# Windowed attention in block-diagonal 64-key tiles, rows divided and then transposed, in front of a squared-ReLU feed-forward layer

## The chip, the cores and the metric

The kernel runs on one core of one Trainium2 chip. The metric is device time in microseconds (us), the median of several executions.

A core has five engines that each work off their own list of instructions: TensorE (PE in the profile; its weight loads are PEld), VectorE (DVE), ScalarE (ACT), GpSimd (POOL) and SyncE (SP; here it only issues transfers). Transfers run on 16 DMA engines. The "granted clock" is the TensorE clock in parts of full speed, as the profile records it.

## The reference

There are 8 batches of 8 heads, 576 positions each, head size 64. A position attends to positions at most 32 away. The result, as 4608 tokens of 512, goes through a feed-forward layer with a squared ReLU.

```python
scores = q @ k.T / sqrt(64)
mask   = abs(pos[:, None] - pos[None, :]) <= 32
attn   = softmax(where(mask, scores, -1e9))
x      = (attn @ v)            # then (batch, position, head*64): 4608 x 512
h      = x @ w_in              # 512 -> 2048
g      = s * maximum(h, 0)**2 + b
out    = g @ w_out             # 2048 -> 512, float32
```

The kernels compute `b` apart: `g @ w_out = s*(r*r @ w_out) + b*colsum(w_out)`. The column sum is a vector that is needed before the first output row.

## The kernel before

Everything is bf16 on TensorE. The work comes as tasks, each with a stream (its engine), a guessed cost, the tiles that it reads and writes, and a priority `key`. A small planner in the kernel's own program goes through the tasks as a simulated machine would and so fixes, when the kernel is built, one order of instructions for each engine. Nothing in the program changes these orders later: each engine is given its list as it stands, with waits at semaphores in it. The costs in the planner therefore cost no time themselves; they only decide orders.

```python
# the planner: take the task that can start first; ties go by key
for s in self.STREAMS:
    for t in open_[s]:
        c = (max(free[s], t.ready), t.key, t.n)
        if best is None or c < best[0]:
            best = (c, t)
...
if t.dma is not None:                       # one queue for all transfers
    dma_free = max(dma_free, st + 1300.0) + t.dma[1]
    t.fin = dma_free + 700.0
```

Attention goes in units of 192 queries and two pairs of heads, six units a batch. Per unit: scores (keys stationary), exp, a mask multiply, then two groups of matmuls with the probabilities moving: one with a matrix of ones (the row sums) and one with V. The sums come out in the layout of the result, so log, exp(-x) and a multiply give x already transposed for the feed-forward layer.

```python
add("act", exp(SC) -> EX)                       # 128 x 1024
add("dve", EX *= MASK)
for (dst, res) in ((SS, "SS"), (AV, "AV")):     # ones, then V, stationary; EX moving
    add("pe", 8 matmuls: dst[64*hh:..., ...] <- lhsT = ONES or VB, rhs = EX)
add("act", LNS = ln(SS));  add("act", REC = exp(-LNS))
add("dve", XT = AV * REC)
# ... a unit of batch b > 0 may not be planned before a chosen feed-forward step:
r = 32 + 6 * (i - 3) - 7 + 3 * g2               # cut: i counts 192-row blocks
after = [("s1", r // 16, r % 16)]
```

q, k and v are loaded as float32, cast on VectorE, and q and k are transposed by DMA (by TensorE for batch 0). The feed-forward layer goes in blocks of tokens, 384, 128 and then 512 each: `s1` is x times `w_in`, ScalarE does the ReLU, VectorE the square, `s2` is the second matrix, VectorE scales and adds, SyncE stores.

The softmax here doesn't subtract the row's maximum and nothing guards it: scores larger than these inputs give would overflow.

## Time and profile before

| | before |
|---|---|
| time, median of 3 runs | 371.59 us (369.63 to 373.37) |
| span of the profiled execution | 373.8 us |
| TensorE busy | 319.2 us |
| ScalarE / VectorE / GpSimd busy | 206.4 / 193.2 / 44.7 us |

First the page of the kernel before: the busy line, and the span in 40 slices (each digit is a busy share in tenths; PEclk is the granted clock).

```profile
PE 319.2 (85%) x2385; PEld 155.5 (42%) x2424; DVE 193.2 (52%) x439; ACT 206.4 (55%) x310; POOL 44.7 (12%) x62
PE   1277985935499999988898899989999999999996
PEclk9999998975599999999999999999999999999999
DMA  8979999999999999999899798863000001001012
```

TensorE is idle at the start and in a hole at slices 9 to 11, where its clock falls too; DMA is nearly full until slice 27 (about 250 us) and then idle. The same by stretches of time: for each stretch its length, then the busy time of each engine with its count of instructions, the granted clock, the DMA share and GB/s.

```profile
0.00:34.00 34.00, 14.42 (x151) 9.33 (x152) 15.55 (x44) 14.08 (x20) 6.75 (x17) 1.00 1.01 164
80.00:106.00 26.00, 14.36 (x135) 8.09 (x137) 15.21 (x34) 13.51 (x20) 5.99 (x7) 0.56 1.20 222
140.00:240.00 100.00, 92.34 (x786) 43.89 (x797) 63.42 (x145) 70.84 (x105) 10.18 (x12) 1.00 1.06 186
```

And the hole, in TensorE's timeline (start, duration, what, and the idle time before it with what ended it):

```profile
84.11 0.64 PE L458 MATMUL ss<-ex,ones 128*64 128x128 bf16 x8 [2.03 <-DVE ex L445]
84.54 0.63 PE L458 MATMUL av<-ex,vb 128*64 128x128 bf16 x8
85.11 0.61 PE L435 MATMUL sc<-qt,kt 64*128 64x128 bf16 x8
87.65 0.64 PE L458 MATMUL ss<-ex,ones 128*64 128x128 bf16 x8 [1.93 <-DVE ex L445]
```

One unit every 3.6 us, nothing else to run: TensorE waits for the exp and mask of each unit, and there is no feed-forward work because block 2 needs batch 1. The Trainium skill ("TensorE: Matmul & The Clock Gate", section "HAM oscillation — how this bites in real kernels") says that idle gaps of TensorE of more than some 3.4 us bring its clock down; here pauses of 2 us between bursts of some 1.6 us already go with a granted clock of 0.56.

### The profile page before, as it was taken

To read this page: it belongs to the slowest core of one execution; us is meant where nothing else is said; L and a number is where in the kernel's file an instruction comes from. 1 tells how busy PE (TensorE), PEld (TensorE's weight loads), DVE (VectorE), ACT (ScalarE), POOL (GpSimd) and SP (SyncE) were. 2 spreads that over 40 slices of the span, in tenths; PEclk is the share of its full clock that TensorE was granted. 3 is DMA by queue.
4 is the path that set the end of the run, shared out by engine and by line. 5 is a ranking of instruction groups with operands and counts; after the bars stand their busy time and mean duration, and the time that the engine had idled before them with its cause. 6 is when DMAs were issued, how large, how long until landed. Compare 5 with 4: busy or idle time off the path is not lost.

```text
span 373.8 us, 6108 instructions
## 1 busy us (share of the span) xinstructions
PE 319.2 (85%) x2385; PEld 155.5 (42%) x2424; DVE 193.2 (52%) x439; ACT 206.4 (55%) x310; POOL 44.7 (12%) x62
## 2 busy tenths in 40 slices
PE   1277985935499999988898899989999999999996
PEld 0144543523244444443444344434444444444442
DVE  4363525745556775676585586454444453333321
ACT  1266732255368678767677576657676764434300
POOL 3012241342221210121111000000000000000000
PEclk9999998975599999999999999999999999999999
DMA  8979999999999999999899798863000001001012
GB/s 164 208 110 187 190 225 206 202 190 213 230 221 147 180 200 231 186 198 193 188 172 213 132 174 174 189 141 89 28 31 31 28 30 56 28 30 56 28 58 84
DMA packets 127869, 52.71 MB, mean 141 GB/s; under 512 B 116672, under 2 KB 120768, under 8 KB 127840
## 3 DMA queue, kind: packets, MB, share of 16 engines
q1 hardware_dynamic: 113648, 36.32, 54.2%
q0 software_dynamic: 7424, 14.29, 19.8%
q10 hardware_dynamic: 6768, 1.70, 2.7%
q8 instruction: 19, 0.31, 0.4%
q14 instruction: 10, 0.08, 0.1%
HBM read 38.80 MB, written 9.44 MB: 129 GB/s over the span
## 4 chain that ended last, share of the span: by engine, by line
PE 54%; DMA 19%; SPq 9%; DVE 7%; ACTq 3%; ACT 3%; issue 2%; DVEq 0%
PE o L543 25%; PE w L525 22%; DMA stgq<-in_q_dram 12%; DMA stgk<-in_k_dram 7%; SPq L300 6%; ACTq L300 3%; SPq L387 3%; PE ss L458 3%; PE sc L435 2%; DVE ex L445 2%; PE av L458 2%; ACT ex L442 1%; DVE xt L472 1%; DVE vb L379 1%; DVE gt L534 1%
## 5 line engine op out<-in xcount | busy, mean ns | idle before, releaser
L525 PE MATMUL w<-xt,win 128*128 128x512 bf16 (+2 forms) x624 | 146.4, 367 | 5.5 <-DVE xt L472 4.2
L543 PE MATMUL o<-wout,gt 128*128 128x512 bf16 x554 | 141.5, 382 | 6.0 <-DVE cvec L567 4.0
L525 PEld LDWEIGHTS w<-xt,win 128*128 128x128 bf16 x640 | 59.4, 100 | 71.8 <-issue 5.1
L543 PEld LDWEIGHTS o<-wout,gt 128*128 128x128 bf16 x576 | 53.2, 98 | 65.5 <-DVE cvec L567 4.2
L442 ACT ACTIVATE ex<-sc,zero 128x1024 bf16<-128x1024 f32 x48 | 53.2, 1109 | 12.1 <-PE sc L435 12.1
L445 DVE TENSOR_TENSOR ex<-ex,mask 128x1024 bf16<-128x1024 bf16 x48 | 33.0, 688 | 33.2 <-ACT ex L442 32.7
L300 POOL DMA_DIRECT2D stgv<-in_v_dram x42 | 35.7, 853 | 120.5 <-DVE vb L379 111.5
L465 ACT ACTIVATE lns<-ss,zero 128x384 f32<-128x384 f32 x48 | 27.7, 578 | 27.6 <-PE ss L458 27.5
L531 ACT ACTIVATE r_29<-w,zero 128x512 bf16<-128x512 f32 (+2 forms) x40 | 25.7, 643 | 30.7 <-PE w L525 30.6
L458 PE MATMUL ss<-ex,ones 128*64 128x128 bf16 x384 | 22.1, 244 | 20.5 <-DVE ex L445 20.1
L531 ACT ACTIVATE r_28<-w,zero 128x512 bf16<-128x512 f32 (+2 forms) x40 | 25.7, 642 | 23.1 <-PE w L525 22.6
L531 ACT ACTIVATE r_31<-w,zero 128x512 bf16<-128x512 f32 (+2 forms) x40 | 25.7, 644 | 23.0 <-PE w L525 22.0
L531 ACT ACTIVATE r_30<-w,zero 128x512 bf16<-128x512 f32 (+2 forms) x40 | 25.7, 643 | 19.2 <-PE w L525 18.8
L555 DVE SCALAR_TENSOR_TENSOR outs<-o,sb_36,cvec 128x512 f32<-128x512 f32 x36 | 26.8, 746 | 13.2 <-PE o L543 12.8
L472 DVE TENSOR_TENSOR xt<-av,rec 128x384 bf16<-128x384 f32 x48 | 26.5, 552 | 11.5 <-ACT rec L468 11.2
L379 DVE CAST natq<-stgq 128x512 bf16<-128x512 f32 (+1 forms) x40 | 17.2, 432 | 25.3 <-DMA stgq<-in_q_dram 25.0
L458 PEld LDWEIGHTS ss<-ex,ones 128*64 128x64 bf16 x384 | 13.6, 119 | 39.6 <-DVE ex L445 26.7
L468 ACT ACTIVATE rec<-lns,zero 128x384 f32<-128x384 f32 x48 | 29.3, 610 | 0.8
L435 PE MATMUL sc<-qt,kt 64*128 64x128 bf16 x384 | 21.2, 237 | 9.0 <-ACT qt L407 5.3
L534 DVE TENSOR_TENSOR gt<-r_29 128x512 bf16<-128x512 bf16 (+2 forms) x40 | 15.8, 396 | 22.7 <-ACT r_29 L531 22.7
L534 DVE TENSOR_TENSOR gt<-r_31 128x512 bf16<-128x512 bf16 (+2 forms) x40 | 15.8, 396 | 22.3 <-ACT r_31 L531 22.0
L534 DVE TENSOR_TENSOR gt<-r_30 128x512 bf16<-128x512 bf16 (+2 forms) x40 | 15.8, 394 | 18.6 <-ACT r_30 L531 18.6
(43 smaller groups left out, 134.4 us busy)
## 6 DMA issues: line engine op xcount, KB each, us to landing
out_dram<-outs SPq DMA_DIRECT2D x36, 256.0 KB, 2.3
stgq<-in_q_dram SPq DMA_DIRECT2D x31, 256.0 KB, 5.8
stgk<-in_k_dram SPq DMA_DIRECT2D x29, 256.0 KB, 6.0
stgv<-in_v_dram POOLq DMA_DIRECT2D x28, 256.0 KB, 5.7
stgv<-in_v_dram POOLq DMA_DIRECT2D x14, 192.0 KB, 5.9
win<-in_moe_w_in_dram POOLq DMA_DIRECT2D x4, 512.0 KB, 6.4
wout<-in_moe_w_out_dram POOLq DMA_DIRECT2D x4, 512.0 KB, 5.8
stgq<-in_q_dram SPq DMA_DIRECT2D x8, 128.0 KB, 5.9
```

The costliest lines, as they stand in the source:

```text
L300: lambda e: e.dma_start(STG[n][p0:p1, blk, :].rearrange("p (h d) -> p h d", h=H), src_of[n][b, :, s0:s0 + ns, :].rearrange("h s d -> s h d ...
L435: fns.append(lambda e, u=u, pr=pr, a=a, hh=hh: e.matmul(SC[:, hh, 256 * u + 128 * a:256 * u + 128 * a + 128], lhsT=KT[slot][64 * hh:64 * h ...
L442: add("act", lambda e: e.activation(EX[e_][:, :, :], SC[:, :, :], AF.Exp, bias=ZERO_F[:, :], scale=0.125), 1130.0, reads=["SC", "ZERO"], w ...
L445: add("dve", lambda e: e.tensor_tensor(EX[e_][:, :, :], EX[e_][:, :, :], MASK[:, :, :], ALU.mult), 700.0, reads=[("E", e_), "MASK"], write ...
L458: fns.append(lambda e, u=u, a=a, hh=hh, dst=dst, lhs=lhs: e.matmul(dst[64 * hh:64 * hh + 64, 192 * u + 64 * a:192 * u + 64 * a + 128], lhs ...
L465: add("act", lambda e: e.activation(LNS[e_][:, :], SS[:, 0:384], AF.Ln, bias=ZERO_F[:, :], scale=1.0), 600.0, reads=["SS", "ZERO"], writes ...
L468: add("act", lambda e: e.activation(REC[e_][:, :], LNS[e_][:, :], AF.Exp, bias=ZERO_F[:, :], scale=-1.0), 600.0, reads=[("LNS", e_), "ZERO ...
L472: add("dve", lambda e: e.tensor_tensor(XT[:, prs[0]:prs[1] + 1, x0:x0 + 192], AV[:, 0:384].rearrange("p (u c) -> p u c", u=2), REC[e_][:, ...
L525: add("pe", [lambda e, kc=kc: e.matmul(W[wb][:, 0:nt], lhsT=WIN_BF[:, kc, ft * 128:(ft + 1) * 128], rhs=XT[:, kc, t0:t0 + nt], start=(kc = ...
L531: add("act", lambda e: e.activation(R1[rb][:, 0:nt], W[wb][:, 0:nt], AF.Relu, bias=ZERO_F[:, :], scale=1.0), 280 + 0.82 * nt, reads=[("W", ...
L534: add("dve", lambda e: e.tensor_tensor(GT[gs][:, ft, 0:nt], R1[rb][:, 0:nt], R1[rb][:, 0:nt], ALU.mult), 160 + 0.53 * nt, reads=[("R1", rb ...
L543: add("pe", [lambda e, fc=fc: e.matmul(O[ob][:, :], lhsT=GT[gs][:, fc, sub * 128:sub * 128 + 128], rhs=WOUT_BF[:, fc, :], start=(fc == 0), ...
```

## The change

The intent is fewer and fuller instructions for attention. Keys and V of two heads are put into block-diagonal 128 x 128 tiles of 64 keys (`KBD`, `VBD`), zero elsewhere. In the second product the probabilities are now the stationary operand and V moves, with a column of ones beside it for each head; so sums and results arrive together, with queries on partitions. A reciprocal of 8 columns and one multiply divide the rows; the result `XN` is then transposed, by TensorE for batch 0, by DMA for the others. V is loaded straight into `VBD` with a cast in the transfer. A batch has five units (128 keys, all heads) in place of six. The column sum moves from TensorE to GpSimd. The first token block has 128 tokens. The pins that tie attention to a feed-forward step are gone; every task has a due time instead, and the planner's model of the DMA gets two queues and new constants.

```diff
-    sizes = [384, 128]
+    sizes = [128, 384]
...
-                dma_free = max(dma_free, st + 1300.0) + t.dma[1]
-                t.fin = dma_free + 700.0
+                me = "sw" if t.stream == "pool" else "hw"
+                other = ring["hw" if me == "sw" else "sw"]
+                at = max(ring[me], st + t.cost + 500.0)
+                ring[me] = at + t.dma[1] + min(t.dma[1], max(0.0, other - at) / 2)
+                t.fin = ring[me] + 1100.0
...
+        def due(b, m):                      # cut: when block of unit m should start
+            return PH[blk] - 14.0 - (1.0 - f) * before
...
+                # q, k of a 128-row chunk, batches 1 to 7
+                add("sp", load STG,  600.0, key=key - 20 + 0.1 * i, ...)
+                add("dve", NAT = cast(STG), 620.0, key=key)
+                add("sp", QT, KT = transpose(NAT), 1250.0, dma=("t", ns * 6.5), key=key)
+                add("dve", KBD = KT in blocks, 260, key=key)
...
-                for (dst, res) in ((SS, "SS"), (AV, "AV")): ...   # ones and V stationary
-            add("act", ... AF.Ln ...);  add("act", ... AF.Exp, scale=-1.0)
-            add("dve", XT = AV * REC)
+                    fns.append(matmul(AVN[0:nr, pr, 0:130], lhsT=EX[...], rhs=VBD[slot][:, j, pr, 0:130]))
+            add("dve", REC = reciprocal(AVN[:, :, 128:130]), 220)
+            add("dve", XN = AVN * REC, 680)
+                add("sp", lambda e: e.dma_start(XT[:, :, x0:x0 + nr], XN[xi][0:nr, :], transpose=True),
+                    1250.0, reads=[("XN", xi)], writes=[("XT", b, m)], key=key, dma=("t", nr * 6.5))
...
-                        r = 32 + 6 * (i - 3) - 7 + 3 * g2
-                        after = [("s1", r // 16, r % 16)]
```

## The prediction

> **What bounds the kernel now.** By time, three different things. The chain of waits and the windows give: 0 to 32 us, no feed-forward matmul runs (loads and the first attention units); 32 to 60 us, TensorE is busy 23 of 28 us and waits for the column-sum vector, whose weights land late because weight loads queue behind batch 0; 75 to 99 us, TensorE is busy 9 of 24 us at a granted clock of 0.58: six attention units of batch 1 run one after the other, about 3.5 us each (exp 1.11, mask 0.69, sums, log 0.58, exp 0.61, multiply 0.55), with no feed-forward work left to fill in. From 99 to 240 us TensorE is busy 94% beside DMA engines that are nearly full; after 240 us it is the only limit. Necessary TensorE work, from start-to-start times in the timeline: 1152 feed-forward matmuls, four in 0.86 us, = 249 us; 48 attention units at about 0.75 us = 36 us; column sum 3.4; transposes about 2: near 291 us of a 374 us span. So about 80 us is loss, two thirds of it before 100 us.
>
> **What the change does to each engine.** TensorE: attention becomes 36 + 52 matmuls of about 128 columns a batch. The trace issues 128-column matmuls, each with new weights, every 55 ns, so 4.9 us a batch, 39 us in all: no gain over 36. The output transposes of batch 0 add 1 to 2 us, the column sum saves 2.5. Total stays near 294 us. ScalarE: log and reciprocal-exp (28 + 29 us) go, exp falls from 53 to some 37 us; it was not the limit except in the serial units. VectorE: V casts (20 us) go, key-block copies and reciprocals come: about equal. GpSimd: 15 adds; the Trainium skill ("GPSIMD Engine Reference", Elementwise) gives 2.6 cycles an element, an estimate of 1.1 us each against the 0.7 that the schedule assumes; no trace here shows it yet. DMA: V is read once, not 1.22 times, already cast; but 35 more DMA transposes come, an estimate of 0.8 to 0.9 us of DMA time each. Per batch some 30 us of DMA against some 36 us of TensorE: nearly full, still hidden.
>
> **The gain is the order, not the arithmetic.** The first block has 128 tokens, weights start at once, attention is placed by due times a block ahead, and 5 units a batch replace 6. I expect the first feed-forward matmul near 20 us (was 31.9), no wait like that of 75 to 99 us (about 20 us back), a shorter wait for the column sum (about 5), some waits left near 45 to 60 us while batch 1 loads beside the weights. Then TensorE runs nearly solid: 20 + 285 + 18 of waits + 5 of drain = 328 us.
>
> **Prediction:** 328 us, 8 in 10 between 312 and 349. Faster by over 2%: 0.95; within 2%: 0.03; slower: 0.02.
>
> **What would show it.** Right: first feed-forward matmul before 24 us; TensorE busy about 90% from 60 us on with the clock at full; ScalarE busy down by about 65 us; VectorE within 10%; attention matmuls about 55 ns apart; GpSimd adds over 1 us. Wrong, if TensorE has a wait of over 10 us after 60 us.
>
> **What would make it wrong.** V's cast load writes 128-byte pieces; if it takes twice the estimated DMA time, DMA binds to the end (345 us or more). The SyncE queue now issues 105 transposes at 1.2 us each, the outputs and all q and k loads in one fixed order, and an output transpose waiting at its head blocks the rest. Slow weight loads for 96-row tiles would add a few us. If all this stays hidden, 312 us.

## The result and the profile after

| | before | after |
|---|---|---|
| time, median (4 runs each) | 372.48 us (369.63 to 377.95) | 386.25 us (385.54 to 386.79) |
| ratio | | 1.039, 95% interval 1.033 to 1.046 |
| span of the profiled execution | 373.8 us | 385.0 us |
| first feed-forward matmul | 31.9 us | 33.8 us |
| start of block 2 (needs batch 1) | 98.8 us | 106.3 us |
| start of block 6 | 229.8 us | 246.4 us |

A ratio is the mean time of one kernel's runs over that of the other's of the same rounds, so not quite the ratio of the medians. Executions over 1.5% slower than the fastest of the same kernel are left out of the means. The kernel became 3.9% slower where 12% less was predicted. The same views as before:

```profile
PE 312.3 (81%) x1948; PEld 167.6 (44%) x1982; DVE 200.5 (52%) x463; ACT 130.1 (34%) x220; POOL 86.4 (22%) x108
PE   3137396971298779887999599999999999999996
PEclk9999699996579989999899799999999999999999
DMA  9999999859968996999889987592121111101012
```

```profile
0.00:34.00 34.00, 11.96 (x98) 9.52 (x99) 15.77 (x39) 9.84 (x12) 32.55 (x46) 1.00 1.31 189
80.00:106.00 26.00, 7.59 (x66) 4.85 (x65) 11.25 (x26) 3.37 (x5) 6.25 (x8) 0.69 1.18 153
140.00:240.00 100.00, 89.41 (x532) 45.82 (x542) 59.43 (x143) 35.29 (x57) 12.45 (x16) 0.94 1.03 172
```

The work did shrink: ScalarE's busy time fell by 76 us, TensorE's by 7. But the hole at 80 to 106 us got deeper (7.6 us of TensorE work in place of 14.4), and the pauses between 140 and 240 us did not close: 10.6 us of pauses where the kernel before had 7.7, now with a clock of 0.94. The loss can be put in three parts: the time before 34 us, TensorE's busy time after it (the sum over the stretches less the first), and the rest.

| us | before | after |
|---|---|---|
| until 34 us | 34 | 34 |
| TensorE busy after 34 us | 304.7 | 300.3 |
| TensorE idle after 34 us | 35.1 | 50.7 |

So the 11.2 us that the span grew by are 15.6 us more idle time, less 4.4 us of work. (In both traces 1 to 2% of the matmul records are missing, 2385 matmuls beside 2424 weight loads before and 1948 beside 1982 after, so the split is good to some microseconds only.)

Where does the idle time come from? What VectorE waited for between 60 and 300 us (total, times, longest, in us). First the kernel before, then after; only the waits for transfers are shown.

```profile
DVE natq L379 <- DMA stgq<-in_q_dram: 13.9, 14, 2.2
DVE natk L379 <- DMA stgk<-in_k_dram: 8.8, 10, 2.0
```

```profile
DVE kbd L429 <- DMA kt<-nat: 22.1, 16, 3.6
DVE nat L420 <- DMA stg<-in_k_dram: 20.5, 14, 2.4
DVE xn L496 <- DMA xt<-xn: 7.1, 7, 2.1
```

What do these waits hold up? Block 2 of the feed-forward layer needs the transposed results of units 0 to 3 of batch 1. Unit 3's rows (`xn`) were ready at 88.66 us. This is what SyncE issues then (start, duration, what):

```profile
88.62 0.57 SPq L393 DMA_DIRECT2D stg<-in_k_dram  x1
...
90.61 1.81 SPq L424 DMA_TRANSPOSE qt<-nat  x1
92.47 1.39 SPq L424 DMA_TRANSPOSE kt<-nat  x1
93.90 1.27 SPq L512 DMA_TRANSPOSE xt<-xn  x1
...
97.53 2.86 SPq L576 DMA_DIRECT2D out_dram<-outs  x1
100.43 1.23 SPq L512 DMA_TRANSPOSE xt<-xn  x1
```

The transpose of unit 2 goes out at 93.90 (its rows were ready 10.7 us before), that of unit 3 at 100.43, 11.8 us late: in SyncE's list, five loads, a pair of transposes for batch 2, unit 2's late transpose and a store stand in front of it. It lands at 106.2 us, and only then block 2 can start. VectorE's list, too, has prefetch in front of due work. VectorE is only 52% busy, so a wait there looks harmless; what stands behind it decides:

```profile
90.46 0.20 DVE L493 RECIPROCAL rec<-avn 96x8 f32<-96x8 f32 x1
91.97 0.75 DVE L420 CAST nat<-stg 128x1024 bf16<-128x1024 f32 x1 [1.30 <-DMA stg<-in_k_dram]
92.64 0.67 DVE L470 TENSOR_TENSOR ex<-ex,mask 128x1024 bf16<-128x1024 bf16 x1
95.22 0.69 DVE L420 CAST nat<-stg 128x1024 bf16<-128x1024 f32 x1 [1.91 <-DMA stg<-in_k_dram]
99.56 0.59 DVE L429 COPY kbd<-kt 64x512 bf16<-64x512 bf16 x2 [3.65 <-DMA kt<-nat]
100.95 0.69 DVE L496 TENSOR_TENSOR xn<-avn,rec 96x512 bf16<-96x512 f32 x1 [0.80 <-DMA xt<-xn]
```

The reciprocal of unit 4, the last of batch 1, is done at 90.66 us. The multiply that makes `xn` from it comes ten microseconds later. Two casts and a pair of copies for batch 2, each waiting for a transfer, stand before it in the list. But they alone do not set this time: at the end the multiply waits 0.80 us more for its buffer. There are two `XN` buffers, and unit 2's transpose, issued late at 93.90, holds this one until it lands; without the casts and copies the multiply would have stood as long. Here it is SyncE's list that binds (such waits are the 7.1 us of `xn L496` above). Whether VectorE's list would hold the multiply by itself can be seen only beside another list on SyncE (section 5 of the experiments). The Trainium skill ("PSUM — Partial Sum Buffer", section "Engine vs sequencer instructions") says that the queues of ScalarE, VectorE and GpSimd are strictly first in, first out; no trace here shows an exception. TensorE in the same stretch:

```profile
89.05 0.62 PE L485 MATMUL avn<-vbd,ex 128*96 128x130 bf16 x8
97.76 1.03 PE L451 MATMUL sc<-qt,kbd 128*128 128x128 bf16 x8 [8.09 <-DMA qt<-nat]
101.69 1.10 PE L485 MATMUL avn<-vbd,ex 128*96 128x130 bf16 x8 [2.90 <-DVE xn L496]
106.26 3.59 PE L544 MATMUL w<-xt,win 128*128 128x512 bf16 x8 [3.47 <-DMA xt<-xn]
```

It waits for a transpose of batch 2 that its own list has next, then for VectorE's late `xn` (which still holds the PSUM tile), then for SyncE's late `xt`: 14.5 us in three pieces.

From 40 to 240 us SyncE is busy issuing for some 19 of every 20 us (18.8 to 19.6): a transpose keeps it 1.26 us in the median (1.40 in the mean, 105 of them), a load 0.59. The outcome is that the plan and the chip drift apart. The kernel's own planner, with the constants that it has, ends at 338 us, with the transpose of unit 3 of batch 1 issued at 74.1 us; on the chip it is issued at 100.4.

Two theories:

- **Orders.** The change's instructions are good, but the orders were planned with transfers that land too early. On the chip the lists of VectorE, SyncE and TensorE then put prefetching, and work that waits for it, in front of work that is due.
- **Amounts (the rivals).** The change simply added too much of something: 35 more DMA transposes on SyncE, V in 128-byte pieces (packets of the software queue rose from 7,424 to 42,112, and the time that they took from 19.8% to 29.0% of the 16 engines' span), weights that block batch 1's loads.

### The profile page after: what moved, and what is told of

The parts are those of the page before. It is cut to its first block, busy times and chain, and to the rows that moved or that the text cites. A ratio compares the mean times of both kernels' runs of the same rounds, so it can differ in the third digit from the quotient of the medians.

```text
span 385.0 us, 5293 instructions
## 1 busy us (share of the span) xinstructions
PE 312.3 (81%) x1948; PEld 167.6 (44%) x1982; DVE 200.5 (52%) x463; ACT 130.1 (34%) x220; POOL 86.4 (22%) x108
## 3 DMA queue, kind: packets, MB, share of 16 engines
q0 software_dynamic: 42112, 8.92, 29.0%
## 4 chain that ended last, share of the span: by engine, by line
PE 51%; DMA 21%; SPq 13%; POOL 7%; DVE 5%; issue 2%; ACT 1%; POOLq 0%; DVEq 0%; ACTq 0%
PE o L561 23%; PE w L544 22%; DMA xt<-xn 7%; SPq L424 7%; DMA stg<-in_k_dram 7%; PE avn L485 4%; DMA kt<-nat 4%; POOL vbd L380 3%; SPq L393 3%; DMA win<-in_moe_w_in_dram 3%; SPq L512 2%; POOL csum L582 2%; PE sc L451 2%; DVE gt L552 1%; DVE nat L420 1%
## 5 line engine op out<-in xcount | busy, mean ns | idle before, releaser
L550 ACT ACTIVATE r<-w 128x512 bf16<-128x512 f32 (+2 forms) x160 | 88.4, 554 | 173.2 <-PE w L544 143.5
L552 DVE TENSOR_TENSOR gt<-r 128x512 bf16<-128x512 bf16 (+2 forms) x160 | 66.5, 424 | 64.9 <-ACT r L550 64.3
L380 POOL DMA_DIRECT2D vbd<-in_v_dram x64 | 49.4, 800 | 168.0 <-PE avn L485 132.6
L485 PE MATMUL avn<-vbd,ex 128*128 128x130 bf16 (+1 forms) x416 | 35.2, 241 | 19.8 <-DVE ex L470 10.4
L468 ACT ACTIVATE ex<-sc 128x1024 bf16<-128x1024 f32 (+2 forms) x48 | 36.4, 773 | 42.8 <-PE sc L451 38.8
L485 PEld LDWEIGHTS avn<-vbd,ex 128*128 128x128 bf16 (+1 forms) x416 | 30.6, 117 | 30.4 <-DVE ex L470 14.4
L420 DVE CAST nat<-stg 128x1024 bf16<-128x1024 f32 (+1 forms) x35 | 25.3, 722 | 26.6 <-DMA stg<-in_k_dram 26.5
L451 PE MATMUL sc<-qt,kbd 128*128 128x128 bf16 (+1 forms) x288 | 23.5, 226 | 14.0 <-DMA qt<-nat 12.3
L470 DVE TENSOR_TENSOR ex<-ex,mask 128x1024 bf16<-128x1024 bf16 (+2 forms) x48 | 25.1, 529 | 17.7 <-ACT ex L468 17.2
L429 DVE COPY kbd<-kt 64x512 bf16<-64x512 bf16 (+1 forms) x70 | 21.0, 300 | 22.6 <-DMA kt<-nat 22.1
L573 DVE SCALAR_TENSOR_TENSOR outs<-o,sb,cvec 128x512 f32<-128x512 f32 x36 | 26.8, 745 | 11.2 <-PE o L561 11.2
L496 DVE TENSOR_TENSOR xn<-avn,rec 128x512 bf16<-128x512 f32 (+1 forms) x40 | 27.4, 686 | 7.6 <-DMA xt<-xn 7.1
L451 PEld LDWEIGHTS sc<-qt,kbd 128*128 128x128 bf16 x288 | 19.4, 103 | 22.4 <-DMA qt<-nat 13.4
L582 POOL TENSOR_TENSOR csum<-csum,wout 128x512 f32<-128x512 f32 x14 | 16.5, 1177 | 1.2
## 6 DMA issues: line engine op xcount, KB each, us to landing
win<-in_moe_w_in_dram POOLq DMA_DIRECT2D x4, 512.0 KB, 10.7
wout<-in_moe_w_out_dram POOLq DMA_DIRECT2D x4, 512.0 KB, 18.8
```

The source lines that it names most:

```text
L380: add("pool", lambda e: e.dma_start(VBD[b % 2][p0:p0 + 64, :, h // 2, p0:p0 + 64], v[b, h, :, :].rearrange("(t p) d -> p t d", p=64)), 900 ...
L420: add("dve", lambda e: e.tensor_copy(NAT[ni][0:ns, :, :], STG[si][0:ns, :, :]), 620.0, reads=[("STG", si, 0), ("STG", si, 1)], writes=[("N ...
L451: fns.append(lambda e, j=j, pr=pr, lo=lo, hi=hi, c0=c0: e.matmul(SC[:, j % 2, pr * 128 + c0:pr * 128 + c0 + hi - lo], lhsT=KBD[slot][:, pr ...
L468: add("act", lambda e, src=src, dst=dst: e.activation(dst, src, AF.Exp, bias=0.0, scale=0.125), 190 + 0.833 * nn * w, reads=["SC"], writes ...
L485: fns.append(lambda e, pr=pr, buf=buf, row=row, col=col, j=j, x=x, last=len(parts) - 1: e.matmul(AVN[0:nr, pr, 0:130], lhsT=EX[buf][:, row ...
L496: add("dve", lambda e: e.tensor_tensor(XN[xi][0:nr, :].rearrange("p (a b c) -> p a b c", a=4, b=2), AVN[0:nr, :, 0:128].rearrange("p a (b ...
```

## The experiments

All kernels gave a correct result within the comparison, the second one too although it leaves V out (attention's share of the result is small, so correctness says little there). Times are medians; "before" is the kernel before.

### 1. Amounts: four runs with the change's planner

The kernel before ran in 373.94 us.

**Transposes of the result on TensorE.** Into spare columns of the same PSUM tile, then a ScalarE copy; no DMA transpose of `XN` is left.

```diff
-                add("sp", lambda e: e.dma_start(XT[...], XN[xi][0:nr, :], transpose=True), 1250.0, ...)
+                add("pe", [4 transposes of XN into AVN's spare columns], 4 * 58.0, ...)
+                add("act", lambda e: e.copy(XT[...], view[:, :, 0:nr]), 600, ...)
```

> The 35 output transposes of batches 1 to 7 leave the SyncE queue and go to TensorE (4 transposes a unit, into spare columns of the attention accumulator) and ScalarE (one copy). Theory S, that the full SyncE queue is the cause (19 of every 20 us busy from 40 to 240 us; an output row waits 4 to 12 us for its transpose to be issued): the first matmul of the third block moves from 106 us to 85 to 92 us, and the whole takes 355 to 370 us against 386, although TensorE gets 8 us more work. Theory V, that the cast loads of V and the DMA engines are the cause: at most 5 us faster, as only 4 MB of 50 go. Theory W, that the start (weights ahead of batch 1) is the cause: the third block still begins after 100 us, and the total stays above 378 us.

Measured: 376.85 us (376.49 to 378.47), ratio to before 1.009 (1.001 to 1.017). It takes back 9.4 of 13.8 us. Block 2 starts at 89.4 us, 17 us earlier than in the changed kernel, but by the end half of that is lost again. Of the expectations only theory S's time for that block (85 to 92 us) was met; the total fits none of the three.

**Less of V.** From batch 2 on, only one of nine key tiles is loaded (a wrong result).

```diff
-                VBD[b % 2][p0:p0 + 64, :, h // 2, p0:p0 + 64],
-                v[b, h, :, :]...
+                VBD[b % 2][p0:p0 + 64, 0:(1 if b > 1 else NTILE), h // 2, p0:p0 + 64],
+                v[b, h, 0:(64 if b > 1 else S), :]...
```

> Wrong result on purpose: from batch 2 on each V load brings one key tile of nine, so 8 of 9 of these packets go; the same instructions in the same order. Theory V: batches 2 to 7 have some 10 us of DMA less each, the total falls by 10 to 30 us. Theories S and W: the total changes by less than 4 us (380 to 387 us), because the SyncE queue issues as many loads and transposes as before.

Measured: 374.73 us (373.56 to 376.52), ratio 1.004 (0.997 to 1.011). Here nothing but DMA traffic went, and 11.5 us came back, as theory V expected.

**The loads of q and k issued by GpSimd** (batches 2 to 7), to relieve SyncE.

```diff
-                add("sp", load STG, 600.0, ..., dma=("l", ns * 9.4))
+                add("pool" if b > 1 else "sp", load STG, 900.0 if b > 1 else 600.0, ..., dma=("q" ...))
```

> Same bytes, same transposes: only the q and k loads of batches 2 to 7 are issued by GpSimd in place of SyncE (still float32, no cast). It takes about 60 issues of 0.6 us or more, some 40 us, off the SyncE queue. Theory S: 8 to 20 us faster than the change as it is (366 to 378 us), third block earlier by 5 to 12 us. Theory V (DMA engines): no gain, within 4 us of 386, since the DMA engines move the same data. Theory W: no gain, as batch 1 is loaded as before.

Measured: 395.07 us (392.99 to 403.24), ratio 1.056: slower, where theory S expected 8 to 20 us less than the change. SyncE had some 43 us less of loads to issue, but the transposes then kept it longer each, 1.65 us in the mean, and filled it again.

**The second weights later**, after batch 1's loads.

```diff
-                for i in range(4): wts.append(load_weights("out", i, -10.0 + i))     # with the first weights
+            if b == 1:                                                               # after batch 1's loads
+                for i in range(4): wts.append(load_weights("out", i, ...))
```

> The second weight matrix is loaded after the q and k loads of batch 1, which no longer queue beside it. Theory W: batch 1's loads land 10 to 15 us earlier, the third block begins at about 92 us and the total falls by 10 to 15 us. Theory S: batch 1 lands earlier, but the queue stays full, so the gain is given back by 240 us in part: total 378 to 386 us, with output rows still waiting 4 us and more for issue. Theory V: less than 4 us.

Measured: 386.5 us (385.39 to 387.99), ratio 1.036: nothing. Block 1 starts 8 us earlier (44.7 us), block 2 at 106.5 as in the changed kernel.

What follows: making transfers fewer helps, which both theories allow, since earlier landings shorten every wait. Against the kernel before, less of V takes back nearly all of the 3.9% that were lost, and the transposes on TensorE three quarters of it; so these runs do not decide between the theories. Experiment 2 does, where all the amounts stay.

### 2. Orders: the same instructions, another plan

For this run not an instruction of the change is altered, only the planner's constants: a transpose keeps SyncE 1.4 us instead of 1.25 (the trace: 1.40 in the mean), transfers take 1.1 to 1.2 times as long, a third transfer in flight blocks SyncE until the first of them lands, and loads beside weight transfers are slow (the trace: batch 1's first two landed at 36.0 and 42.0 us, 10.9 and 16.5 us after issue; planned were 29.8 and 32.2). A comparison of the lists shows that GpSimd's order stayed the same, and that the other four hold the same instructions in another order.

```diff
-                ring[me] = at + t.dma[1] + min(t.dma[1], max(0.0, other - at) / 2)
+                d = t.dma[1] * {"l": 1.1, "v": 1.2, "t": 1.2}.get(t.dma[0], 1.0)
+                if me == "sw":   x = min(0.5 * d, max(0.0, ring["hw"] - at))
+                elif at < wend:  x = min(4.0 * d, wend - at)       # beside the weights
+                else:            x = min(d, max(0.0, ring["sw"] - at))
+                ring[me] = at + d + x
+                if me == "hw":                                     # issue blocks behind two transfers
+                    hist.append(ring[me])
+                    free[t.stream] = max(st + t.cost, hist[-3] - 500.0)       # cut: when there are three
...
-                        1250.0, reads=[("NAT", ni, i)], ...         # both kinds of transposes
+                        1400.0, reads=[("NAT", ni, i)], ...
```

> Exactly the instructions of the change; only the constants from which its fixed order is planned are set nearer to the trace of the change: transposes issue in 1.4 us, loads that stand behind weight loads take up to five times as long, V and transposes 1.2 times the DMA time, an issue blocks when two transfers stand before it. Theory O (the order, planned for transfers that land too early, makes every in-order engine wait at its head): 8 to 20 us faster than the change (366 to 378 us), third block before 97 us, and waits of an output row for its issue well below the 5 to 12 us of the change. Theories S and V (too much work for the queue and the DMA engines, whatever the order): within 4 us of 386.

Measured: **353.75 us** (352.79 to 355.31), ratio to before **0.940** (0.935 to 0.945; before 375.86). The same instructions run 32.5 us faster, more than theory O expected (366 to 378 us); its start of the third block, before 97 us, was missed by little (98.5). Its views, for the same stretches:

```profile
80.00:106.00 26.00, 16.95 (x124) 11.76 (x125) 15.38 (x38) 7.31 (x11) 5.96 (x8) 0.61 0.96 120
140.00:240.00 100.00, 100.00 (x661) 53.37 (x660) 67.03 (x158) 42.77 (x69) 17.66 (x24) 1.00 1.17 171
```

```profile
DVE nat L433 <- DMA stg<-in_k_dram: 4.9, 8, 1.1
DVE kbd L442 <- DMA kt<-nat: 3.1, 4, 1.1
```

VectorE's waits for transfers fell from 49.7 to 8.0 us (22.1 + 20.5 + 7.1; 4.9 + 3.1), and TensorE now works 100 of the 100 us between 140 and 240. DMA moves the same bytes and is busier in that stretch (a share of 1.17 against 1.03), so its capacity did not hold the changed kernel. The good order also prefetches *later*: the last q and k transposes of batch 7 are through at 279 us instead of 252. In VectorE's timeline at the place shown above, the order is now the other way round:

```profile
93.05 0.20 DVE L506 RECIPROCAL rec<-avn 96x8 f32<-96x8 f32 x1 [1.19 <-PE avn L498]
93.29 0.69 DVE L509 TENSOR_TENSOR xn<-avn,rec 96x512 bf16<-96x512 f32 x1
93.90 0.58 DVE L442 COPY kbd<-kt 64x512 bf16<-64x512 bf16 x2
94.51 0.82 DVE L433 CAST nat<-stg 64x1024 bf16<-64x1024 f32 x1
```

The multiply of unit 4 follows its reciprocal at once; the copies and the cast of the prefetch come after it, and by then their transfers have landed. SyncE's list changed in the same sense: the transposes of units 0 to 4 of batch 1 are issued 0.0, 0.7, 0.0, 2.3 and 4.2 us after their rows are ready; in the changed kernel it was 9.7, 10.2, 10.7, 11.8 and 8.8.

### 3. In the same call: amounts again, under a good order, and one part in the kernel before

> e1 (output transposes on TensorE) with the order planned from the same nearer constants. Theory O with S: better than either alone, 358 to 368 us, TensorE waits of over 3 us between 100 and 240 us gone. S alone: as e1, 374 to 380 us.

```diff
# experiment 2, and in it the edit of the first run of section 1
-                add("sp", lambda e: e.dma_start(XT[...], XN[xi][0:nr, :], transpose=True), 1400.0, ...)
+                add("pe", [4 transposes of XN into AVN's spare columns], 4 * 58.0, ...)
+                add("act", lambda e: e.copy(XT[...], view[:, :, 0:nr]), 600, ...)
```

The result's transposes on TensorE, planned anew: 359.24 us as the median of four. One of the four, the profiled execution, was an outlier of 677.2 us, so its trace is not used, and the fast runs count: 358.12, 358.52 and 359.95, with 358.52 in the middle. Ratio 0.954. Expected was better than either edit alone; it is not better than experiment 2.

> e9 and the k transposes of batches 1 to 7 on TensorE too: SyncE issues 35 transposes in place of 105, TensorE does some 8 us more, ScalarE and VectorE evict from PSUM. Theory S: the queue has slack by 150 us, 350 to 362 us, limited by TensorE (about 311 us of work after a start at 34 us). If the loads (DMA engines) are what is left: no better than e9.

```diff
-                add("sp", KT = transpose(NAT[k]), 1400.0, ...);  add("dve", KBD = KT in blocks, 260), twice
+                add("pe", [4 transposes of NAT[k] into SC], 4 * 58.0, ...)
+                add("act", KBD = SC in blocks, 600);  add("dve", KBD = SC in blocks, 430)
```

The same with k's transposes on TensorE as well: 360.77 us (360.05 to 363.2), ratio 0.960.

So the edit that took back 9.4 us under the bad order costs 4.8 us under the good one (358.52 against 353.75). The DMA transposes by themselves were not the cause; moving them was a way round late transfers. With that gone TensorE has more to do: after 34 us it is busy for 307.3 us in the run with k's transposes too, against 297.5 us in experiment 2.

> One part of the change alone, in the kernel before: V of batches 1 to 7 is cast in its load (GpSimd, 128-byte pieces per head), so 42 VectorE casts of 0.42 us go; the rest as before. Theory V (these cast loads are dear for the DMA engines): slower than before by 4 to 15 us. If the cast loads are cheap: same or up to 4 us faster than before (VectorE has 18 us less).

V cast in the load, in the kernel before: 383.55 us (378.21 to 385.07), ratio 1.015 (1.007 to 1.023). The saving of the casts on VectorE does not pay there by itself. By the medians it is 8 us slower, as theory V expected: under the plan of the kernel before, whose costs for these loads were left as they were, the edit costs time (the record's verdict is unclear).

```diff
-                    STG[n][p0:p1, blk, :]...
+                    (VB[b % 2] if vc else STG[n])[p0:p1, blk, :]...      # vc: V of batches 1 to 7
```

### 4. Controls of the plan

The kernel before ran in 375.81 us.

> The kernel before, with the same kind of transfer model in its planner (transposes 1.4 us to issue, 1.1 times the DMA time, slow loads behind weight loads, an issue that blocks behind two transfers); the same instructions. If only the order makes the kernel with the new attention 354 us, and the attention itself gives nothing, this one falls as well, to 350 to 360 us. If the order of the kernel before is not what holds it, it stays within 2% of 373 us; then the new attention is worth what lies between.

```diff
-                dma_free = max(dma_free, st + 1300.0) + t.dma[1]
-                t.fin = dma_free + 700.0
+                d = t.dma[1] * 1.1              # cut: then the two queues as in experiment 2
-                1300.0, reads=[("NAT", n, blk)], ...
+                1400.0, reads=[("NAT", n, blk)], ...
```

The kernel before, planned with the same kind of constants (the guesses for issuing a load are lowered with them, from 1070 to 600 ns on SyncE): 377.69 us (376.72 to 379.83), ratio 1.006. It gains nothing.

> Control in the opposite direction: the change with DMA times in its plan at 0.8 to 0.85 of what they were, further from the trace. The same instructions. Theory O: the prefetch is planned still earlier, the waits at the head of the queues grow, 388 to 405 us. If any other order would have done as well as e8 (luck): 350 to 380 us.

```diff
+                d = t.dma[1] * {"l": 0.85, "v": 0.8, "t": 0.8}.get(t.dma[0], 1.0)
-                ring[me] = at + t.dma[1] + min(t.dma[1], max(0.0, other - at) / 2)
+                ring[me] = at + d + min(d, max(0.0, other - at) / 2)
```

The changed kernel planned the wrong way, with DMA times 0.8 to 0.85 of what they were: 389.33 us (387.07 to 390.11), ratio 1.036. VectorE's waits for loads and k transposes rise from 42.6 to 59.7 us. The time is at the low end of what was expected, and its ratio cannot be told from the change's 1.039: another order is no better, but that a plan further from the trace makes the kernel slower is not shown.

> Of the new constants only the one for the start: loads behind weight loads are slow. If the slip of 19 us that batch 1 picks up there is what spoils the order: 355 to 368 us. If the steady rate matters: 378 to 387 us.

Only the constant for loads beside weights: 387.76 us (385.79 to 389.99), ratio 1.032. Nothing.

```diff
-                ring[me] = at + t.dma[1] + min(t.dma[1], max(0.0, other - at) / 2)
+                x = min(t.dma[1], max(0.0, other - at) / 2)
+                if me == "hw" and at < wend:
+                    x = min(4.0 * t.dma[1], wend - at)
+                ring[me] = at + t.dma[1] + x
```

> Of the new constants all but that one: transposes 1.4 us, DMA times 1.1 to 1.2, the issue blocks behind two transfers. If the steady rate matters: 353 to 362 us, near e8. If the start matters: 375 us and more.

```diff
# against experiment 2
-                    x = min(4.0 * d, wend - at)
+                    x = min(d, max(0.0, ring["sw"] - at))
```

All new constants but that one: 355.97 us (354.99 to 357.78), ratio 0.948. Nearly all of the gain. So it is not the one spectacular error of the plan (16.5 us for one load) that counts, but the others, which bear on each of 105 transposes and 80 loads.

### 5. Whose order?

Here the changed kernel's order is kept, instruction by instruction, on all engines but the named ones; those are planned anew with the nearer constants. Theory for these runs: it is VectorE's list. "Planned" is where the planner, with the nearer constants, sees the end; for the changed kernel's own orders it sees 384.

```diff
         g.plan()                                   # the change's own planner
+        g.plan_part(("dve",))                      # again, nearer constants; the other lists stay
...
+                for t in open_[s]:
+                    if s not in loose and t is not seqs[s][at_[s]]:
+                        continue                   # a kept list: only its next task may start
```

> The changed kernel with only VectorE's order new: that queue is re-planned with the same nearer constants, the other four engines keep their order of the changed kernel, instruction by instruction (compared before sending). Theory: the loss sits in VectorE's in-order queue, where casts of prefetched q and k stand in front of the attention's own work and wait for their loads. Then this alone takes back most of the loss: 366 to 376 us (my own model of the queues gives 372), and VectorE's waits on transfers between 60 and 300 us fall from about 50 to under 20 us. Rival: the order of SyncE carries it; then this is within 2% of 386.

> The same with only SyncE's order new. Theory (VectorE's order carries the loss): no gain, 382 to 392 us. Rival (late issue of loads and transposes carries it, since SyncE is busy 19 of 20 us): 355 to 372 us.

> SyncE's and VectorE's order new, TensorE's, ScalarE's and GpSimd's kept. If the two only work together, this falls by clearly more than the two alone together: 360 to 368 us. If VectorE's order alone does it, it equals the run with VectorE alone within 1.5%.

> Only TensorE's and ScalarE's order new (how attention units and feed-forward blocks are interleaved), VectorE's and SyncE's kept. If the interleaving on TensorE is what counts: 355 to 370 us. If VectorE's queue holds it all the same: 376 to 386 us (my model gives 379).

> TensorE's, ScalarE's and VectorE's order new, SyncE's and GpSimd's kept from the changed kernel. SyncE's new order alone made it slower (398.5 us), VectorE's alone took back 7, TensorE's and ScalarE's alone 4, SyncE's and VectorE's together 16, all together 32 us. If the orders must fit each other: about 370 us (my model of the queues gives 365), so SyncE's order is worth some 15 us here although it cost 12 alone. If the gains of the single engines simply add: 375 us, and then the full re-plan's 354 is still unexplained. If SyncE's order does not matter once the others are new: 354 to 358.

| new order on | planned | measured, us | against 386.25 |
|---|---|---|---|
| none (the change) | 384 | 386.25 | |
| VectorE | 372 | 379.49 (378.36 to 379.87) | -6.8 |
| SyncE | 390 | 398.53 (395.91 to 399.72) | +12.3 |
| TensorE, ScalarE | 379 | 382.70 (382.23 to 383.9) | -3.6 |
| SyncE, VectorE | 364 | 370.30 (369.3 to 371.78) | -16.0 |
| TensorE, ScalarE, VectorE | 365 | 372.88 (369.85 to 373.34) | -13.4 |
| TensorE, ScalarE, VectorE, SyncE | 347 | 353.75 (352.79 to 355.31) | -32.5 |

(The first row and the last two come from other calls than the rest; the kernel before was within 372.5 and 376.5 us in all of them.) The theory that VectorE's list alone carries the loss fell: it takes back 7 us, not the 10 to 20 expected. The rival, SyncE's list, fell harder. New alone it makes the kernel 12 us slower (the planner saw this coming, 390 against 384), and the waits of VectorE show why:

```profile
DVE kbd L495 <- DMA kt<-nat: 38.9, 20, 5.4
DVE nat L486 <- DMA stg<-in_k_dram: 26.0, 13, 3.9
```

SyncE now issues the due transposes sooner (1.0 us after their rows are ready in the mean of the 35, against 3.7 in the changed kernel) and the prefetched chunks later, but VectorE's old list still has the copies and casts of these chunks early, in front of the due work. At the place shown above, unit 4 of batch 1:

```profile
93.85 0.20 DVE L559 RECIPROCAL rec<-avn 96x8 f32<-96x8 f32 x1
97.41 0.99 DVE L486 CAST nat<-stg 128x1024 bf16<-128x1024 f32 x1 [3.36 <-DMA stg<-in_k_dram]
102.88 0.69 DVE L486 CAST nat<-stg 128x1024 bf16<-128x1024 f32 x1 [3.88 <-DMA stg<-in_k_dram]
105.43 0.59 DVE L495 COPY kbd<-kt 64x512 bf16<-64x512 bf16 x2 [1.86 <-DMA kt<-nat]
106.03 0.69 DVE L562 TENSOR_TENSOR xn<-avn,rec 96x512 bf16<-96x512 f32 x1
```

Unit 2's transpose has landed here, so the multiply waits for no buffer; VectorE's list alone holds it, for 12.0 us. In the run with only VectorE's list new it is the other way round, and the buffer that SyncE's old list holds makes it 10.1 us:

```profile
91.54 0.20 DVE L559 RECIPROCAL rec<-avn 96x8 f32<-96x8 f32 x1 [1.09 <-PE avn L551]
101.89 0.69 DVE L562 TENSOR_TENSOR xn<-avn,rec 96x512 bf16<-96x512 f32 x1 [0.76 <-DMA xt<-xn]
```

With both new the multiply follows its reciprocal at once.

With VectorE's list free as well, freeing SyncE's is worth 9 us (379.49 to 370.30), and with all others free 19 us (372.88 to 353.75). These are not one list of SyncE in different company: in each run the planner makes the free lists anew around the kept ones, and SyncE's lists in the rows "SyncE" and "SyncE, VectorE" differ in 155 of 222 places. So the table tells what it is worth to free a list, not what experiment 2's list of one engine does alone; that was not run. The single gains add up to a loss of 1.9 us; together they are a gain of 32.5. (Each against the kernel before, they add up to a gain of 4.1% against 9.9%.) Either way no one list is at fault: **the lists have to fit each other.** The planned ends ran 2 to 9 us low and ranked all seven kernels as the chip did.

### 6. A little further

> The re-planned kernel (353.75 us) with one more constant moved: the loads of q and k get a priority 15 us ahead of their due time in place of 20, so that prefetch competes less with the work that is due. Theory (too early a prefetch costs): 348 to 352 us (model 344 against 347). Rival (the lead does not matter any more): within 1% of 353.75.

```diff
-                    600.0, writes=[("STG", si, i)], key=key - 20 + 0.1 * i, dma=("l", ns * 9.4),
+                    600.0, writes=[("STG", si, i)], key=key - 15 + 0.1 * i, dma=("l", ns * 9.4),
```

Measured: 350.13 us (349.49 to 351.47), ratio 0.944 (0.932 to 0.955; before 374.25). The median is 3.6 us below that of experiment 2, the ratios to before cannot be told apart. Both beat the kernel before and the change (the record calls this run's ratio unclear, since four of the seven runs of the kernel before count as slow there; but each of its own runs is below each of those). This one has the lowest time.

## Why the prediction was wrong

Predicted 328 us (312 to 349), measured 386.25. By its parts:

**The step that failed: "Then TensorE runs nearly solid: 20 + 285 + 18 of waits + 5 of drain = 328 us."** Measured terms, from the stretches:

| us | predicted | after | re-planned (experiment 2) |
|---|---|---|---|
| before the first feed-forward matmul (cut at 34 us in both) | 20 | 34 | 34 |
| TensorE work after it | 285 | 300 | 297 |
| TensorE idle after it, with drain | 23 | 51 | 22 |

- *Waits and drain, 23 us.* This is the largest miss, 28 us, and the runs show its cause: orders that do not fit when the transfers land, planned with constants that have them land too early. In the re-planned kernel, with the same instructions, the term is 22. (297.5 = 309.9 less 12.4 before 34 us; 21.5 is what remains of the 353.0 us.) "The gain is the order" was right as a sentence. The mistake was to take the new order as the diff intends it, due times and all, and not to ask whether the planner's constants for transfers agree with the trace. The trace of the kernel before had the material: transposes 1.49 us each in the mean on a SyncE that was already full.
- *The start, 20 us.* Measured 33.8, and 33.4 in the re-planned kernel. The order does not cure it. In the trace after, VectorE stands at the casts of batch 0's last chunk until 22 us while the first `xn` waits behind them; and GpSimd's clearing of the block-diagonal tiles takes 2.0 us a piece where the plan has 1.3, and the first piece is on the chain that ended last (most of GpSimd's 7% there is the issue of V's loads and the column sum). Neither was tested.
- *The work, 285 us.* 15 us more after 34 us, of which some is the lower clock after pauses (0.945 in the mean) and some the modelled ends of matmuls; not split further.

Point by point:

- "No wait like that of 75 to 99 us": wrong, it was deeper. Even the re-planned kernel has TensorE busy only 17 of 26 us there, at a clock of 0.61.
- "Wrong, if TensorE has a wait of over 10 us after 60 us": the waits of 8.09, 2.90 and 3.47 us before block 2 are that wait, in pieces; no single one reaches 10 us.
- "The SyncE queue now issues 105 transposes at 1.2 us each ... in one fixed order": named as a risk, and near the truth. But it feared that an output transpose would wait at the head of the list and block the rest. The reverse happened: finished rows stood 10 us behind prefetch. And it was not SyncE's list alone, but its fit with VectorE's and TensorE's.
- "DMA ... nearly full, still hidden": in capacity it was right (the re-planned kernel moves the same bytes), in the time of landing it was not.
- "V's cast load writes 128-byte pieces": it was no limit by itself; with the same loads the re-planned kernel runs in 354 us.
- ScalarE down by about 65 us: 76. VectorE within 10%: 200.5 against 193.2. Attention matmuls 55 ns apart: 56 to 57. Slow weight loads for 96-row tiles: 137 ns in the mean against 109 for 128 rows. GpSimd adds over 1 us: 1177 ns in the mean of 14 and 1149 for the first, so the estimate of 1.1 us from the Trainium skill ("GPSIMD Engine Reference", Elementwise) held and the schedule's 0.7 did not. A shorter wait for the column sum: 2.1 us, it was 4.0.

What the change itself is worth, as far as one new plan for each kernel tells, is 353.75 against 377.69 us, or 6%; the bad fit of its orders cost 32 us and hid it. Why the kernel before does not mind its planner's constants was not tested; its pins hold attention at fixed feed-forward steps whatever the DMA model says, which could be the reason.

Still open: which of the three constants of the fourth control (issue time, transfer times, blocking behind two transfers) does the work; what holds the first feed-forward matmul at 33 us; and the hole before block 2, which starts at 98.5 us in experiment 2 and at 94.4 in the last.

## What to carry to other kernels

When a static schedule is changed, check its cost constants against the trace before trusting any gain "from the order": compare planned and measured times of a few landings, not only of busy engines. Put prefetch work into a first-in, first-out list only behind the due work that it could hold up, and judge a wait on a half-idle engine by what stands behind it in that list. Move the lists of the engines together: a new order on one queue alone can make the kernel slower, as it did here by 12 us.

## What the Trainium skill lacked or had wrong

- "DMA: Bandwidth & Descriptors", section "Issuing engines are not separate DMA queues", says that the sequencer time to start a DMA is "usually small relative to the DMA itself". Here a DMA transpose of a 128 x 512 bf16 tile keeps SyncE 1.26 us in the median (1.18 at least) and lands 2.6 to 3.8 us after issue in the median; with these, the loads and the stores SyncE is busy issuing for some 19 of every 20 us between 40 and 240 us. For a transpose between on-chip tiles the page has an issue time only for 8,192 tiles on unnamed "previous generations"; I found none for one tile of this size on this chip.
- The same page, section "Queues, rings and completion order", has the engines take turns between queues packet by packet. No page says what that does to a load beside large transfers of the software queue: 10.9 and 16.5 us from issue to landing, against 4.4 to 4.8 in the median.
- "TensorE: Matmul & The Clock Gate", section "Back-to-back issue gap", gives a sustained 81 ns a matmul for 128 columns and 131 ns for 512 with new weights each time. The traces here show 56 to 57 ns and 216 ns in the median (four in 0.22 and in 0.86 us), which is what the page calls the isolated gap.
- "PSUM — Partial Sum Buffer", section "Engine vs sequencer instructions", has the strict order of VectorE's queue in one sentence. I found no page that draws the consequence that mattered here: in the run with only SyncE's list new, the waits of a prefetch at the head of that queue held finished work for 12.0 us (94.05 to 106.03 us) on an engine that is 50% busy.
